# Attention and two MLPs on one core: keys and queries turned by VectorE, softmax sums spread through DRAM

## The chip, the cores and the metric

The kernel runs on one core of a Trainium2 chip. The metric is the device time of one execution in microseconds (us). A core has five engines that run side by side, each with its own instruction list in order: PE (TensorE, matmuls; PEld is its weight load), DVE (VectorE), ACT (ScalarE), POOL (GpSimd) and SP (SyncE, which here issues nearly all DMAs). They wait for each other by semaphores.

## The reference

Inputs are q, k, v (4 batches, 8 heads, 576 tokens, 64 wide), tau, and two pairs of MLP weights of 512x2048 and 2048x512.

```python
scores = scale * np.matmul(q, k.transpose(0, 1, 3, 2))
thresh = np.max(scores, axis=-1, keepdims=True) - tau
scores = np.where(scores >= thresh, scores, -1000000000.0)
attn = np.exp(scores - np.max(scores, axis=-1, keepdims=True))
attn = attn / (np.sum(attn, axis=-1, keepdims=True) + 1e-09)
x = np.matmul(attn, v)          # then (batch, token, head * width): 2304 x 512
h = x @ w_in                    # MLP 1: g = h >= 1: h; h <= -1: 0; else (h + 1)**2 / 4
x = g @ w_out
h = x @ moe2_w_in               # MLP 2: g = h * clip(h + 3, 0, 6) / 6
out = g @ moe2_w_out
```

## The kernel before

**Attention.** The 16 jobs are pairs of heads of one batch (job = 4 x batch + pair). A job's 576 queries go in five blocks, four of 128 and one of 64 (step t is one block, five steps a job). For each job `load_q` and `load_k` bring the two heads' rows to `qn`, `kn` with tokens on the partitions; `unit_q` and `unit_k` turn them on PE (five and six transpositions with `ident` into a pair of PSUM banks P0/P1, line 254) and ACT copies them to `qt`, `kt` (L266, L277; the copy of q also scales by `taus[:, 1:2]`, 0.125 where tau is not negative). A block is: `em_scores`, PE multiplies `qt` by `kt` into a P bank (L296), and DVE negates the scores to SBUF and keeps the row's smallest (L309); `em_exp`, ACT's exponential (L320), and DVE's threshold `th`, one instruction for each head (L322); `em_mask`, DVE zeroes what is beyond the threshold and sums the row into a column of `zt` (L328); `em_pt` and `em_tail`, PE turns the block's probabilities, nine transpositions into banks Q0/Q2 and Q3, from the moment MLP work is let in all into Q0, and ACT copies them out (L352, L355, L366, L370); `pv_chunk`, ten pairs of matmuls with `vn` into Q1 (L388), copied to `xu` by ACT (L394).

**The norm.** When a job's five blocks are summed, `pre_norm` takes the reciprocals `rz` (L408) and POOL spreads them 64 wide to `rb` (L412). Four steps later `em_norm` turns `rb` and `rz` on PE (five transpositions, L426 and L429) and DVE multiplies `xu` by the result (L431, L437). `xu` goes to DRAM (`xd`) and to the MLP.

**MLP 1 beside the attention.** Each f32 matrix is held as two f32r halves, so each product is three matmuls. `em_h` (L633) and `em_part` (L695) work on 256 tokens. The weights come as 64-bit numbers and are split by ACT, POOL and DVE (L116 to L139). The attention is a generator; from the step in which job 3's norm is done (`ready(0)`), each of its `yield` points adds 0.57 to a credit, and MLP 1 pieces are emitted while the credit is positive (L892 to L909). Behind the attention the rest of MLP 1 and MLP 2 run alone (L633 and L675).

**Order.** The program emits in this order, and a scheduler then places each engine's instructions by priority; some edges are set by hand (`after`). DMAs of SP run in SP's order: an issue that waits holds those behind it. `qn` and `kn` are single buffers, so the next job's load is issued when the turn of the present one has read them.

Of the kernel before, what the change touches and what calls it, by code (L numbers as in the profile page):

```python
# [18 lines left out]
def kernel(  # L19
# [12 lines left out]
    nc = tc.nc  # L32
# [15 lines left out]
    NF1 = 10  # L48
    MLAG = 2
# [161 lines left out]
    def rows(src):  # L211
        return src[0:MAIN, :].rearrange("(p c) d -> p c d", c=4)

    def load_q(j):
# [4 lines left out]
        for h in HEADS:  # L219
            src = q[b, 2 * hp + h]  # L220
            E.dma_start(out=qn[:, 0:4, h * D:(h + 1) * D], in_=rows(src))
            E.dma_start(out=qn[0:TAIL, 4, h * D:(h + 1) * D], in_=src[MAIN:SEQ, :])

    def load_k(j):
# [3 lines left out]
        for h in HEADS:  # L228
            src = k[b, 2 * hp + h]
            nc.sync.dma_start(out=kn[:, 0:4, h * D:(h + 1) * D], in_=rows(src))  # L230
# [3 lines left out]
    def load_v(j):  # L234
# [4 lines left out]
        for h in HEADS:  # L239
            src = v[b, 2 * hp + h]  # L240
            nc.sync.dma_start(out=t[:, 0:4, h, :], in_=rows(src))
# [16 lines left out]
    def unit_q(j):  # L258
        if j >= NJ or j in qt:
            return  # L260
        tm = unit_bank().rearrange("p e n -> p (e n)")
# [3 lines left out]
        qt[j] = ap.tile([128, SEQ], F32, tag="qt", name="qt", bufs=2)  # L265
        reads(S.activation(out=qt[j], in_=tm[:, 0:SEQ], func=ACTF.Copy, scale=taus[:, 1:2]))  # L266

    def unit_k(j):

        if j >= NJ or j in kt:  # L270
            return
        tm = unit_bank().rearrange("p e n -> p (e n)")
# [3 lines left out]
        kt[j] = ap.tile([128, SEQ + TAIL], F32, tag="kt", name="kt", bufs=2)  # L276
# [5 lines left out]
    def em_scores(j, i):  # L282
# [25 lines left out]
        for x, s in enumerate(ss):  # L308
            reads(V.tensor_scalar(out=p[:, x], in0=s[:, :, 0:HS], scalar1=-1.0, scalar2=3e38,  # L309
# [5 lines left out]
    def em_exp(j, i, x):  # L315
        p, nm, th, es = blk[j, i]
        if x >= (1 if i == NBLK - 1 else 2):
# [4 lines left out]
        V.tensor_scalar(out=th[:, x:x + 1], in0=nm[:, x:x + 1], scalar1=taus[:, 0:1], scalar2=None, op0=ALU.add)  # L322
# [17 lines left out]

    def em_pt(j, i, h):
# [5 lines left out]
        tm = bank("Q0" if mode["mlp"] or mode["n"] % 2 else "Q2")  # L347
# [10 lines left out]
    def em_tail(j, i):  # L358
# [4 lines left out]
        tl = bank("Q0" if mode["mlp"] else "Q3")  # L363
# [11 lines left out]
    def pv_chunk():  # L375
# [4 lines left out]
        if c == 0:  # L380
# [3 lines left out]
            o_t[j, g] = bank("Q1")  # L384
# [17 lines left out]
    def pre_norm(j):  # L402
# [14 lines left out]
    def em_norm(j):  # L417
# [5 lines left out]
        rz, rb = rbs.pop(j)  # L423
        bm = unit_bank().rearrange("p e n -> p (e n)")
# [580 lines left out]
```

## Time and profile before

| | |
|---|---|
| median of 3 runs | 1137.3 us (1137.07 to 1139.17) |
| span of the profiled execution | 1136.9 us |
| PE busy | 1108.0 us (97%) |
| PE weight load busy | 901.2 us (79%) |
| DVE busy | 575.6 us (51%) |
| ACT busy | 632.6 us (56%) |
| POOL busy | 404.3 us (36%) |
| DMA | 80.09 MB, mean 70 GB/s |

Busy times are shares of the whole span, but the program has stages with different loads, so they are read again for each stage below. An engine that is busy less than the bound can still hold it up, if a wait for it ends last. Matmuls overlap in PE, so the time that a group costs is read from the starts of its neighbours. The profiled execution's span and the runs' median differ by 0.4 us.

### The profile page before, as it was taken

To read this page: it belongs to the slowest core of one execution; us is meant where nothing else is said; L and a number is where in the kernel's file an instruction comes from. 1 tells how busy PE (TensorE), PEld (TensorE's weight loads), DVE (VectorE), ACT (ScalarE), POOL (GpSimd) and SP (SyncE) were. 2 spreads that over 40 slices of the span, in tenths; PEclk is the share of its full clock that TensorE was granted. 3 is DMA by queue.
4 is the path that set the end of the run, shared out by engine and by line. 5 is a ranking of instruction groups with operands and counts; after the bars stand their busy time and mean duration, and the time that the engine had idled before them with its cause. 6 is when DMAs were issued, how large, how long until landed. Compare 5 with 4: busy or idle time off the path is not lost.

```text
span 1136.9 us, 18024 instructions
## 1 busy us (share of the span) xinstructions
PE 1108.0 (97%) x6680; PEld 901.2 (79%) x6680; DVE 575.6 (51%) x1272; ACT 632.6 (56%) x1239; POOL 404.3 (36%) x383
## 2 busy tenths in 40 slices
PE   7998899999999999999999999999999999999998
PEld 5665567778777788788889988888888888898886
DVE  5888887766565565445545756557511111121111
ACT  5787987866666666556566766645432222333222
POOL 0222676411111111136645765557622222222221
PEclk8999999999999999999999999999999999999999
DMA  6434335222111210015322344533110110010001
GB/s 161 106 77 102 109 108 151 63 81 71 47 49 32 53 43 13 11 34 167 98 75 93 117 143 150 184 111 111 38 42 1 32 38 1 10 38 1 19 1 38
DMA packets 105368, 80.09 MB, mean 70 GB/s; under 512 B 66368, under 2 KB 90176, under 8 KB 105280
## 3 DMA queue, kind: packets, MB, share of 16 engines
q1 hardware_dynamic: 103920, 78.64, 23.9%
q8 instruction: 53, 0.87, 0.3%
q10 hardware_dynamic: 1360, 0.30, 0.1%
q14 instruction: 35, 0.29, 0.1%
HBM read 61.60 MB, written 17.30 MB: 69 GB/s over the span
## 4 chain that ended last, share of the span: by engine, by line
PE 88%; ACT 4%; DVE 4%; issue 1%; DMA 1%; POOL 1%; ACTq 0%; SPq 0%; DVEq 0%
PE Q L633 34%; PE P L675 27%; PE Q L695 7%; PE P L296 7%; PE Q L388 6%; PE Q L254 5%; DVE p L309 2%; ACT e L320 1%; PE P L254 1%; DVE p L328 1%; ACT Gf L352 1%; PE P L426 0%; POOL w_c L135 0%; DMA w_raw<-in_moe_w_in_dram 0%; DVE xl L617 0%
## 5 line engine op out<-in xcount | busy, mean ns | idle before, releaser
L651 POOL TENSOR_TENSOR gl<-r,gh 128x512 fp32r<-128x512 f32 (+1 forms) x190 | 203.3, 1071 | 548.4 <-ACT gh L650 547.9
L633 PE MATMUL Q<-xh,wih 128*128 128x512 f32 (+1 forms) x760 | 263.2, 346 | 2.5 <-DVE r L644 2.5
L633 PE MATMUL Q<-xh,wil 128*128 128x512 f32 (+1 forms) x760 | 257.0, 338 | 0.0
L633 PE MATMUL Q<-xl,wih 128*128 128x512 f32 (+1 forms) x760 | 256.8, 338 | 0.0
L647 DVE SCALAR_TENSOR_TENSOR r<-r,Q 128x512 f32<-128x512 f32 (+1 forms) x80 | 50.7, 634 | 249.0 <-ACT r L646 248.9
L650 ACT ACTIVATE gh<-r 128x512 fp32r<-128x512 f32 (+1 forms) x190 | 99.8, 526 | 126.2 <-PE P L675 53.3
L633 PEld LDWEIGHTS Q<-xh,wih 128*128 128x128 f32 x760 | 143.9, 189 | 25.0 <-issue 4.8
L633 PEld LDWEIGHTS Q<-xl,wih 128*128 128x128 f32 x760 | 143.9, 189 | 15.7
L633 PEld LDWEIGHTS Q<-xh,wil 128*128 128x128 f32 x760 | 143.8, 189 | 15.2
L646 ACT ACTIVATE r<-Q,three 128x512 f32<-128x512 f32 (+1 forms) x80 | 51.4, 643 | 143.7 <-PE Q L633 140.6
L309 DVE TENSOR_SCALAR_CACHE_REDUCE p<-P 128x576 f32<-128x576 f32 x144 | 104.3, 754 | 50.2 <-PE Q L254 32.0
L328 DVE SCALAR_TENSOR_TENSOR p<-p,th,e 128x576 f32<-128x576 f32 x144 | 121.3, 860 | 15.7 <-ACT e L320 14.9
L644 DVE SCALAR_TENSOR_TENSOR r<-r,Q 128x256 f32<-128x256 f32 (+1 forms) x110 | 55.0, 500 | 135.1 <-ACT r L643 127.7
L320 ACT ACTIVATE e<-p,nm 128x576 f32<-128x576 f32 x144 | 109.1, 774 | 25.4 <-DVE p L309 24.3
L254 PE MATMUL Q<-ident,p 128*128 128x128 f32 x656 | 109.8, 283 | 11.3 <-ACT Gf L352 4.9
L675 PE MATMUL P<-woh,gh 128*128 128x512 f32 x288 | 112.0, 390 | 0.6 <-DVE ob L733 0.6
L675 PE MATMUL P<-wol,gh 128*128 128x512 f32 x288 | 112.3, 390 | 0.0
L254 PEld LDWEIGHTS Q<-ident,p 128*128 128x128 f32 x656 | 74.5, 141 | 46.3 <-ACT Gf L352 12.7
L675 PE MATMUL P<-woh,gl 128*128 128x512 f32 x288 | 111.0, 390 | 0.0
L296 PE MATMUL P<-kt,qt 64*128 64x288 f32 (+1 forms) x640 | 100.5, 433 | 6.0 <-DVE p L309 4.9
L135 POOL TENSOR_TENSOR w_c<-w_c,w_raw 128x512 int32<-128x512 int32 x64 | 88.6, 1384 | 39.1 <-DVE w_c L133 22.7
L352 ACT ACTIVATE Gf<-Q 128x512 f32<-128x512 f32 x128 | 74.9, 594 | 40.0 <-PE Q L254 39.2
(84 smaller groups left out, 1865.1 us busy)
## 6 DMA issues: line engine op xcount, KB each, us to landing
w_raw<-in_moe_w_in_dram SPq DMA_DIRECT2D x32, 512.0 KB, 4.1
w_raw<-in_moe_w_out_dram SPq DMA_DIRECT2D x32, 512.0 KB, 3.7
kn<-in_k_dram SPq DMA_DIRECT2D x32, 128.0 KB, 2.6
vn<-in_v_dram SPq DMA_DIRECT2D x32, 128.0 KB, 2.9
x2p<-ob SPq DMA_DIRECT2D x16, 256.0 KB, 2.2
x2d<-ob SPq DMA_DIRECT2D x16, 256.0 KB, 4.1
xst<-x2d SPq DMA_DIRECT2D x16, 256.0 KB, 3.3
out_dram<-ob SPq DMA_DIRECT2D x16, 256.0 KB, 2.2
```

Source lines behind the costliest of these rows:

```text
L135: x = G.tensor_tensor(out=c.bitcast(I32), in0=c.bitcast(I32), in1=r, op=ALU.add)
L254: x = T.transpose(out, in_, ident)
L296: mm = T.matmul(o, qt[j][r, c], kt[j][r, k0:k0 + HS], start=True, stop=True, skip_group_check=True)
L309: reads(V.tensor_scalar(out=p[:, x], in0=s[:, :, 0:HS], scalar1=-1.0, scalar2=3e38, op0=ALU.mult, op1=ALU.min, accum_out=nm[:, x:x + 1]), ...
L320: pins["S"] = S.activation(out=e, in_=p[:, x], func=ACTF.Exp, bias=nm[:, x:x + 1], scale=-1.0)
L328: V.scalar_tensor_tensor(out=p[:, x], in0=p[:, x], scalar=th[:, x:x + 1], in1=e, op0=ALU.is_le, op1=ALU.mult, accum_out=zt[j][:, z:z + 1])
L352: S.activation(out=f[:, h, :, d0:d0 + 128], in_=tm.rearrange("p (c n) -> p c n", c=4), func=ACTF.Copy)
L633: mm = T.matmul(h, l[:, kk * 128:(kk + 1) * 128], r, start=(x == 0), stop=(x == 3 * KD - 1))
L650: x = S.activation(out=gh, in_=r, func=ACTF.Copy)
L651: y = G.tensor_tensor(out=gl, in0=r, in1=f32(gh), op=ALU.subtract)
L675: T.matmul(a, l, r, start=(first and x == 0), stop=(last and x == 2))
L695: mm = T.matmul(o, l, r, start=(f == fs[0] and x == 0 and i == 0), stop=(f == fs[-1] and x == 2 and i == 1), skip_group_check=True)
```

## The change

For batches two to four (`NAT = 1`: jobs 4 to 15) q and k are loaded as strips: each DMA fills 32 partitions with 32 of a head's 64 columns, in pieces of 128 bytes, and one DVE instruction turns all 32x32 blocks of q (576 wide), another of k (640 wide), straight into `qt` and `kt`. PE's transpositions and ACT's copies of these jobs go, and with them their use of the P banks. The scale moves to DVE's pass over the scores (a pointer to -0.125 in place of the number -1). The rows of these batches' v and of the output follow in the new token order.

For jobs 4 to 14 (`OVER`) the norm leaves PE: the 128x9 reciprocals are stored to DRAM turned, in pieces of 4 bytes, read back broadcast to 64 partitions each, and POOL multiplies `xu` by them in one instruction.

The two thresholds of a block become one DVE instruction. While MLP work is let in, `em_pt`, `em_tail` and `pv_chunk` all rotate through Q0 and Q1. Two branches of the attention's step for that time become one, with four `yield` points a step where a job had 22 in its five steps.

```diff
+    NAT = 1
     def zcol(x, c):
-        return 8 if c == NBLK - 1 else c // 2 * 4 + x * 2 + c % 2
+        return 8 if c == NBLK - 1 else x * 4 + c
+    OVER = range(HP, NJ - 1)
...
+    def strips(t, s0, src, h):
+        n = src.shape[0] // 32
+        flat = t.rearrange("p c n -> p (c n)")
+        for x in range(2):
+            p0 = 64 * h + 32 * x
+            nc.sync.dma_start(out=flat[p0:p0 + 32, 32 * s0:32 * (s0 + n)].rearrange("p (s d) -> p s d", d=32),
+                              in_=src[:, 32 * x:32 * x + 32].rearrange("(s p) d -> p s d", p=32))
...
     def unit_q(j):
+        qt[j] = ap.tile([128, SEQ], F32, tag="qt", name="qt", bufs=2)
+        if jobs[j][0] >= NAT:
+            V.transpose(out=qt[j], in_=qn.rearrange("p c n -> p (c n)")[:, 0:SEQ])
+            load_q(j + 1)
+            return
...
-        reads(S.activation(out=qt[j], in_=tm[:, 0:SEQ], func=ACTF.Copy, scale=taus[:, 1:2]))
+        reads(S.activation(out=qt[j], in_=tm[:, 0:SEQ], func=ACTF.Copy))
...
     def unit_k(j):
+        if jobs[j][0] >= NAT:
+            V.transpose(out=kt[j], in_=kn.rearrange("p c n -> p (c n)"))
+            load_k(j + 1)
+            return
...
-            reads(V.tensor_scalar(out=p[:, x], in0=s[:, :, 0:HS], scalar1=-1.0, scalar2=3e38,
+            reads(V.tensor_scalar(out=p[:, x], in0=s[:, :, 0:HS], scalar1=taus[:, 1:2], scalar2=3e38,
...
-        V.tensor_scalar(out=th[:, x:x + 1], in0=nm[:, x:x + 1], scalar1=taus[:, 0:1], scalar2=None, op0=ALU.add)
+        if x == n - 1:
+            V.tensor_scalar(out=th[:, 0:n], in0=nm[:, 0:n], scalar1=taus[:, 0:1], scalar2=None, op0=ALU.add)
...
+    def rotate():
+        mode["r"] = 1 - mode.get("r", 0)
+        return bank(f"Q{mode['r']}")
...
-        tm = bank("Q0" if mode["mlp"] or mode["n"] % 2 else "Q2")
+        tm = rotate() if mode["mlp"] else bank("Q0" if mode["n"] % 2 else "Q2")
...
-        tl = bank("Q0" if mode["mlp"] else "Q3")
+        tl = rotate() if mode["mlp"] else bank("Q3")
...
-            o_t[j, g] = bank("Q1")
+            o_t[j, g] = rotate() if mode["mlp"] else bank("Q1")
...
+        if j in OVER:
+            rd = dram.tile([9, 128], F32, name=f"rd{j}")
+            nc.sync.dma_start(out=rd.rearrange("c p -> p c"), in_=rz[:, :, 0])
+            for h in HEADS:
+                r = slice(64 * h, 64 * h + 64)
+                nc.sync.dma_start(out=rb[r, 0:MAIN].rearrange("p (c n) -> p c n", c=4),
+                                  in_=rd[4 * h:4 * h + 4, :].unsqueeze(0).to_broadcast([64, 4, 128]))
+                nc.sync.dma_start(out=rb[r, MAIN:SEQ], in_=rd[8:9, r].to_broadcast([64, 64]))
...
+        if j in OVER:
+            load_v(j + 2)
+            x = xu.pop(j)
+            G.tensor_tensor(out=x, in0=x, in1=rb, op=ALU.mult)
...
-            elif t < 35:
...
                 if t < n:
                     em_scores(*order[t])
                     maskq.append(order[t])
                     em_exp(*order[t], 0)
                     em_exp(*order[t], 1)
+                masked()
                 for x in now_at("z"):
                     pre_norm(*x)
-                masked()
                 yield
+                now = due(1)
+                for b in now:
+                    em_pt(*b, 0)
                 for x in now_at("n"):
                     em_norm(*x)
-                    yield
+                yield
+                pv_run(5)
                 tails(1)
-                pv_run(5)
                 yield
...
```

PE, last block of a job in the third quarter of the attention, before (`qn` are the next job's queries, `rb` and `rz` the former job's reciprocals, `p` the probabilities, the rest MLP 1):

```order
L254 MATMUL P_3574<-ident,qn 128x128 x5
L296 MATMUL P_3622<-kt,qt 64x288 x4
L254 MATMUL Q_3495<-ident,p 128x128 x4
...
L426 MATMUL P_3644<-ident,rb 128x128 x4
L429 MATMUL P_3644<-ident,rz 128x128
L254 MATMUL Q_3505<-ident,p 128x128 x4
L633 MATMUL Q_3501<-xh,wih_1344 128x256
```

The same place now (lines are those of the changed kernel, 323 the scores, 273 a turn, 645 and 707 MLP 1):

```order
L323 MATMUL P_3440<-kt,qt 64x288 x4
L273 MATMUL Q_3338<-ident,p 128x128 x4
L707 MATMUL Q_3198<-gh,woh_2773 128x256
L707 MATMUL Q_3198<-gl,woh_2773 128x256
L707 MATMUL Q_3198<-gh,wol_2774 128x256
L273 MATMUL Q_3380<-ident,p 128x128 x4
L645 MATMUL Q_3374<-xh,wih_1073 128x256
```

The turns of q and of the sums are gone, and those of k a little further on; the turns of `p` and the scores keep their places.

DVE at the same block, before (L431 and L437 are the norm's products, L407 and L408 the sums' reciprocals):

```order
L328 SCALAR_TENSOR_TENSOR p,z<-p,th,e 128x576 x2
L431 TENSOR_TENSOR xu<-xu,P_3644 128x512
L437 TENSOR_TENSOR xu<-xu,P_3644 64x64 x2
L309 TENSOR_SCALAR p,nm<-P_3622 128x576
L322 TENSOR_SCALAR th<-nm,taus 128x1
L644 SCALAR_TENSOR_TENSOR r<-r,Q_3501 128x256
L328 SCALAR_TENSOR_TENSOR p,z<-p,th,e 128x576
```

And now, in such a block (357 the mask, 336 the pass over the scores, 656 MLP 1):

```order
L357 SCALAR_TENSOR_TENSOR p,z<-p,th,e 128x576 x2
L282 STREAM_TRANSPOSE qt<-qn 128x576
L297 STREAM_TRANSPOSE kt<-kn 128x640
L656 SCALAR_TENSOR_TENSOR r<-r,Q_2854 128x256
L336 TENSOR_SCALAR p,nm<-P_3044,taus 128x576
L351 TENSOR_SCALAR th<-nm,taus 128x1
L357 SCALAR_TENSOR_TENSOR p,z<-p,th,e 128x576
```

Where the norm's products stood, the two block turns stand, one block ahead of the next job's first scores.

SP over one job late in the attention, before:

```order
L241 DMA vn_97<-in_v_dram 128x4x64 x2
L242 DMA vn_97<-in_v_dram 64x64 x2
L221 DMA qn<-in_q_dram 128x4x64
L222 DMA qn<-in_q_dram 64x64
...
L434 DMA xd_78<-xu 128x512
L438 DMA xd_80<-xu 128x64
L230 DMA kn<-in_k_dram 128x4x64
L232 DMA kn<-in_k_dram 64x64 x2
```

And now, from a job's loads of q to its last strip of k (`rd` is the sums' place in DRAM, 445 the store, 448 and 450 the broadcasts):

```order
L223 DMA qn<-in_q_dram 32x18x32 x4
L223 DMA kn<-in_k_dram 32x18x32 x2
L223 DMA kn<-in_k_dram 32x2x32 x2
L223 DMA kn<-in_k_dram 32x18x32
L445 DMA rd_2763<-rz 128x9x1
...
L448 DMA rb<-rd_2763 64x512
L450 DMA rb<-rd_2763 64x64
...
L223 DMA kn<-in_k_dram 32x2x32
```

The store and the broadcasts stand between the strips of k, so the last strip is issued behind a wait for the store's landing.

## Rows read from the trace of the kernel before

**Rows 1.** The page, part 1: busy us, share of the span, instructions.
```profile
PE 1108.0 (97%) x6680; PEld 901.2 (79%) x6680; DVE 575.6 (51%) x1272; ACT 632.6 (56%) x1239; POOL 404.3 (36%) x383
```

**Rows 2.** Busy time by stage: start:end, length, each engine's busy us.
```profile
core 0: us, PE busy (x) PEld busy (x) DVE busy (x) ACT busy (x) POOL busy (x), PEclk, DMA share, GB/s
0.00:109.00 109.00, 97.57 (x696) 65.45 (x697) 87.30 (x260) 81.15 (x163) 20.10 (x35) 0.97 0.42 108
109.00:212.00 103.00, 93.56 (x693) 69.61 (x692) 85.87 (x211) 85.23 (x183) 65.69 (x63) 1.00 0.43 122
212.00:472.00 260.00, 256.87 (x1998) 206.23 (x1996) 157.99 (x465) 171.68 (x369) 39.62 (x59) 1.00 0.18 46
472.00:1137.00 665.00, 659.96 (x3303) 559.90 (x3299) 244.40 (x339) 294.55 (x525) 278.93 (x227) 1.00 0.21 66
```

**Rows 3.** PE's waits, 109 to 472 us: us in total, times, longest.
```profile
PE Q L254 <- ACT Gf L352: 4.6, 6, 1.5
...
PE Q L254 <- ACT Gt L366: 1.4, 3, 0.6
...
PE Q L254 <- ACT Gf L355: 0.8, 1, 0.8
```

**Rows 4.** PE in order of time, 300 to 312 us: start, us, instructions.
```profile
300.93 0.71 PE L254 MATMUL P<-ident,qn 128*128 128x128 f32 x5
301.57 1.19 PE L296 MATMUL P<-kt,qt 64*64 64x288 f32 x8
...
304.26 0.60 PE L426 MATMUL P<-ident,rb 128*128 128x128 f32 x4
...
304.81 0.60 PE L254 MATMUL Q<-ident,p 128*128 128x128 f32 x4
...
309.30 0.82 PE L254 MATMUL P<-ident,kn 128*128 128x128 f32 x6
309.96 0.60 PE L254 MATMUL Q<-ident,p 128*128 128x128 f32 x4
```

**Rows 5.** Groups by shape, 109 to 472 us: count, busy us, mean ns, idle before.
```profile
L254 PE MATMUL P<-ident,kn 128*128 128x128 f32 x60 | 8.7, 272 | 0.0
```

**Rows 6.** Groups by shape over the whole span, same columns.
```profile
L651 POOL TENSOR_TENSOR gl<-r,gh 128x512 fp32r<-128x512 f32 x98 | 130.6, 1333 | 270.4 <-ACT gh L650 270.1
...
L328 DVE SCALAR_TENSOR_TENSOR p<-p,th,e 128x576 f32<-128x576 f32 x144 | 121.3, 860 | 15.7 <-ACT e L320 14.9 <-ACT Gt L366 0.3
...
L322 DVE TENSOR_SCALAR th<-nm,taus 128x1 f32<-128x1 f32 x144 | 25.3, 207 | 0.4
...
L266 ACT ACTIVATE qt<-P,taus 128x576 f32<-128x576 f32 x16 | 11.8, 739 | 1.4 <-PE P L254 1.4
...
L277 ACT ACTIVATE kt<-P 128x640 f32<-128x640 f32 x16 | 11.2, 703 | 1.1 <-PE P L254 1.0
...
L431 DVE TENSOR_TENSOR xu<-xu,P 128x512 f32<-128x512 f32 x16 | 11.0, 685 | 16.7 <-PE P L429 10.8 <-ACT xu L394 5.8
```

**Rows 7.** Single lines: ns min/median/max, first and last start in us.
```profile
L408 DVE RECIPROCAL rz<-z x9: 210/216/216, 212.1 to 472.1; 128x9 f32<-128x9 f32 x9
...
L230 SPq DMA_DIRECT2D kn<-in_k_dram x32: 572/588/703, 0.7 to 409.8; - x32
```

**Rows 8.** POOL and DVE in order of time, 126.5 to 130 us.
```profile
127.21 1.78 POOL L139 TENSOR_TENSOR wol<-w_c,woh 128x512 fp32r<-128x512 f32 x1
...
127.80 1.82 DVE L328 SCALAR_TENSOR_TENSOR p<-p,th,e 128x576 f32<-128x576 f32 x1
```

**Rows 9.** DMA issues: count, KB each, median us from issue to landing.
```profile
kn<-in_k_dram SPq DMA_DIRECT2D x32, 128.0 KB, 2.6
...
kn<-in_k_dram SPq DMA_DIRECT2D x64, 16.0 KB, 2.3
...
taus<-in_tau_dram ACTq DMA_DIRECT2D x1, 0.5 KB, 2.9
```

More of the change, by code (lines that the diff above doesn't have):

```diff
@@ L209, with rows @@
     qt, kt = {}, {}
-    def rows(src):
+    def rows(src, b):
+        if b >= NAT:
+            return src[0:MAIN, :].rearrange("(c p) d -> p c d", c=4)
         return src[0:MAIN, :].rearrange("(p c) d -> p c d", c=4)
+    def strips(t, s0, src, h):
[5 more added lines that the diff above has]
+                              in_=src[:, 32 * x:32 * x + 32].rearrange("(s p) d -> p s d", p=32))
     def load_q(j):
@@ L220, in load_q @@
             src = q[b, 2 * hp + h]
-            E.dma_start(out=qn[:, 0:4, h * D:(h + 1) * D], in_=rows(src))
+            if b >= NAT:
+                strips(qn, 0, src, h)
+                continue
+            E.dma_start(out=qn[:, 0:4, h * D:(h + 1) * D], in_=rows(src, b))
             E.dma_start(out=qn[0:TAIL, 4, h * D:(h + 1) * D], in_=src[MAIN:SEQ, :])
@@ L229, in load_k @@
             src = k[b, 2 * hp + h]
-            nc.sync.dma_start(out=kn[:, 0:4, h * D:(h + 1) * D], in_=rows(src))
+            if b >= NAT:
+                strips(kn, 2, src, h)
+                strips(kn, 0, src[MAIN:SEQ, :], h)
+                continue
+            nc.sync.dma_start(out=kn[:, 0:4, h * D:(h + 1) * D], in_=rows(src, b))
             for r in range(2):
@@ L240, in load_v @@
             src = v[b, 2 * hp + h]
-            nc.sync.dma_start(out=t[:, 0:4, h, :], in_=rows(src))
+            nc.sync.dma_start(out=t[:, 0:4, h, :], in_=rows(src, b))
             nc.sync.dma_start(out=t[h * TAIL:(h + 1) * TAIL, 4, h, :], in_=src[MAIN:SEQ, :])
@@ L316, in em_exp @@
         p, nm, th, es = blk[j, i]
-        if x >= (1 if i == NBLK - 1 else 2):
+        n = 1 if i == NBLK - 1 else 2
+        if x >= n:
             return
@@ L423, in em_norm @@
         rz, rb = rbs.pop(j)
+        if j in OVER:
+            load_v(j + 2)
+            x = xu.pop(j)
+            G.tensor_tensor(out=x, in0=x, in1=rb, op=ALU.mult)
+            done_jobs.add(j)
+            if b < NB - 1:
+                nc.sync.dma_start(out=xd[b][:, hp, :], in_=x[:, 0:MAIN])
+            nc.sync.dma_start(out=xd[NB][:, hp, b * TAIL:(b + 1) * TAIL], in_=x[:, MAIN:SEQ])
+            return
         bm = unit_bank().rearrange("p e n -> p (e n)")
@@ L569, in attention @@
                     unit_q(*x)
-                    yield
-                for b in now:
-                    em_pt(*b, 0)
-                    yield
-                pv_run(5)
                 for b in now:
@@ L737, in fin_out @@
             b, r = divmod(c, MAIN // 128)
-            nc.sync.dma_start(out=out[b * SEQ:b * SEQ + MAIN, :].rearrange("(p c) d -> c p d", c=4)[r], in_=ob)
+            if b >= NAT:
+                dst = out[b * SEQ + r * 128:b * SEQ + r * 128 + 128, :]
+            else:
+                dst = out[b * SEQ:b * SEQ + MAIN, :].rearrange("(p c) d -> c p d", c=4)[r]
+            nc.sync.dma_start(out=dst, in_=ob)
         else:
```

52 lines of the change are left out of this document (8 added, 44 removed).

## The prediction, made before the changed kernel was run

> **What bounds the kernel now.** First the page's busy times: PE works 1108.0 us of the 1136.9 us span, the other engines 36 to 56% [rows 1]. The reader is to see that only PE can be the bound as an average. Second, the same by stage, since the change touches one stage alone [rows 2]: to 109 us jobs 0 to 4 of the attention run alone; from 109 to 212 us jobs 5 to 7 run beside the first MLP pieces, and the weights are split there; from 212 to 472 us jobs 8 to 15 run beside MLP pieces with the weights ready; then MLP alone. PE idles 11.4, 9.4, 3.1 and 5.0 us in them. In the third stage PE is busy 99% while DVE and ACT are at 61 and 66%: a PE microsecond removed there is a microsecond of the kernel. In the second DVE and ACT are both busy 83%, in the first 80 and 74% with little else for PE to do: there a shorter PE list can turn into PE waiting. In the last stage PE has nothing to gain or lose but its work. The granted clock is 1.00 from 109 us on. Third, the waits: of PE's idle time from 109 to 472 us, 4.6 + 1.4 + 0.8 = 6.8 us were ended by ACT copying a turned block out of its bank [rows 3].
>
> **Time on the span.** The rows are of an execution with a span of 1136.9 us; the median of the runs is 1137.3, so 0.4 us lies around it. The sum below is a difference and is taken from 1137.3.
>
> **PE work that goes.** 12 jobs (4 to 15) lose 5 turns of q and 6 of k, 11 jobs (4 to 14) lose the 5 turns of the norm: 187 turns. What a turn costs is read from starts, not from durations: from the start of a group to the start of what follows it are 301.57 - 300.93 = 0.64 us for q, 309.96 - 309.30 = 0.66 for k and 304.81 - 304.26 = 0.55 for the norm [rows 4]. So 12 x 1.30 + 11 x 0.55 = 21.7 us. The durations of single turns mislead: 60 turns of k have a mean of 272 ns but keep PE busy 8.7 us together, 145 ns each, because they overlap [rows 5]. The Trainium skill (TensorE: Matmul & The Clock Gate, Part 4: PE-mode transpose) gives about 275 ns for a transposition inside a kernel; the trace agrees with that as a duration, 272 ns, and by it the sum would be 187 x 0.275 = 51 us and the time 1086, an estimate that the starts speak against.
>
> By stage: q and k of jobs 4 and 5 fall before 109 us (2.6 us); q and k of jobs 6 to 8 and the norms of 4 to 6 in the second stage (3 x 1.30 + 3 x 0.55 = 5.6 us); q and k of 9 to 15 and the norms of 7 to 14 in the third (7 x 1.30 + 8 x 0.55 = 13.5 us). I take the third whole. Of the second I take half, 2.8 us, between none (DVE and ACT set the pace) and all. Of the first I take nothing, between 0 and 2.6: there PE waits for DVE, and DVE gets longer. Sum 16.3 us: **1121.0 us**.
>
> **What must hide for that.** *DVE* gets two turns of 32x32 blocks a job, 576 and 640 wide. No row shows one. The nearest is the two-input pass of 512 at 685 ns [rows 6], which scales to 0.77 + 0.86 = 1.6 us; with twice the rate of the mask (860 ns for 576) it is 1.7 + 1.9 = 3.6. I take 1.6, since a plain pass from SBUF to SBUF is nearest to the first row. It loses four threshold instructions of 207 ns and the norm's product, 0.69, so 1.5 a job. Scaling the scores by a pointer in place of -1 may cost something: ACT's copy with a pointer takes 739 ns for 576, without one 703 for 640, which bounds it at 0.11 x 9 = 1.0 us a job. DVE's load in the third stage is 158.0/8 = 19.8 us a job of 32.5 (8 jobs from 212.1 to 472.1 [rows 7]); after it is 19.9 to 22.9 of 30.8. It is hidden there. *ACT* loses two copies, 0.74 + 0.70 = 1.4 us a job: 20 of 30.8. *POOL* trades two small broadcasts for one product of 576, 1.5 us by its row for 512 (1333 ns). It is idle 85% of the third stage, but it shares something with DVE: beside a POOL pass of 1.78 us one DVE mask took 1.82 us where 860 ns is the mean [rows 8]. So each product may cost DVE up to 1.0 us, 11 us in all, and nothing of it on PE's path while DVE has 8 us a job to spare. *SP*: a job issues 4 q, 8 k, 5 for the sums, 4 v and 2 stores, 23 where 16 were; at 588 ns [rows 7] that is 4.1 us more, 13.5 of 30.8.
>
> **The two banks.** Turns now alternate between Q0 and Q1. A turn no longer waits for the copy of the one just before it, so up to 6.8 us can go [rows 3]; but the PV group now takes one of the two banks for its whole length and its copy (685 ns at most, by the DVE row of the same size) stands before the second turn after it: 23 groups stand there in the order, x 0.69 = up to 16 us. PE has MLP matmuls to put between. I take 0, ends of a gain of 7 and a loss of 16, and expect nearer the first.
>
> **Fewer stops for the MLP.** A job now has 20 points at which MLP work is let in, not 22, with 0.57 a point. The orders show it: of the MLP's matmuls 1320 stood among the attention's, now 1179. The 141 others run behind the attention, where PE idles 0.8%. So this is worth nothing by itself; what it costs is cover: a shorter attention with less MLP in it has fewer PE instructions to fill a wait with. In the second stage this is what could eat the other half.
>
> **Rivals.** *All of it and the waits too.* If the free banks take the 6.8 us of copy waits away and stages one and two give their whole share, 21.7 + 6.8: 1108.8. For it: ACT, which ends those waits, loses 1.4 us a job. Against: DVE and ACT at 83% in the second stage.
>
> *DVE and ACT become the bound.* With the block turn at 3.6, the pointer at 1.0 and the POOL product at 1.0, DVE in the second stage goes from 85.9/3 = 28.6 to 32.7 us a job of 34.3, so PE cannot get through faster there, and in the third to 23.9 of 30.8, where each late mask now meets less MLP cover. Then stage two gives nothing and stage three half: -6.8, 1130.5.
>
> *SP holds the keys back (slower).* One mechanism: the sums of a job are stored to DRAM in 1152 pieces of 4 bytes, and SP waits for their landing, L, before it issues their broadcast; the last k strips stand behind that on SP, and DVE turns k in order, so a late strip stops DVE, the scores and PE. From one turn of k to the next are 30.8 us. SP reaches the store after about a block, 6.1 us, issues it (0.6), waits L, issues 4 broadcasts and the last strip (3.0), which lands in 2.6: 12.3 + L. It decides from L = 18.5 us. Rows: 64 pieces (16 KB) land in 2.3 us, 512 pieces (128 KB) in 2.6, and 128 pieces of 4 bytes in 2.9 [rows 9]. By the first pair 1152 pieces cost 0.8 more, L = 3.1; by the last, 0.6/128 each, L = 7.7. Both are far from 18.5. Beyond it each us costs 11: L = 21 gives 27.5 back and 1148.5. The Trainium skill (VectorE: DVE Perf Modes, The three transpose paths) warns that a plain DMA that transposes by strides is 19 times slower than the DMA's own transposition. That speaks against exactly this store; the rows' 2.9 us for pieces of 4 bytes do not, and no run here shows the other path. By 19 times the 2.3 us row L would be 44 us, 25.5 beyond the point, and the time about 1400; of the 0.08 below I give that 0.02.
>
> *It does nothing.* The 16.3 us come back as PE waits of the same length in stages two and three, 1137. It needs about 1 us a job that nothing above names.
>
> **How the numbers follow.** Forecast as worked (1114 to 1127, by the half of stage two, the first stage and a few us for the banks): 0.57. All and the waits (1107 to 1113): 0.15. DVE and ACT the bound (1128 to 1134): 0.16. Nothing: 0.04. SP slower: 0.08. A measurement tells 0.2%, 2.3 us, from no change. So faster 0.88, same 0.04, slower 0.08. The range goes from 1109 to 1131, the ends of the second and third case; it leaves out the slower case, nothing, and parts of two.
>
> **What would show it.** Right: 187 fewer turns; the job in the third stage near 30.8 us by the reciprocals; PE at 98% or more there; the block turns under 1 us each; the sums' store landing under 8 us; q and k landed long before DVE turns them. Wrong: PE waits on the block turns' DMA; block turns of 1.7 us; PE idle from 109 to 212 us well over 9.4 us (the half I gave stage two is gone) or copy waits of PV's bank of more than some us.

## The result, and the profile after

The changed kernel takes 1144.2 us (median of 4 runs, 1142.6 to 1146.6), the kernel before 1137.6 (4 runs): ratio 1.006, interval 1.0048 to 1.0073. It is slower by 7 us, where the forecast was 16 us faster; the time lies above the range. The profiled execution has a span of 1144.8 us, 7.9 more than the 1136.9 of before.

PE did lose work. The page's busy times, beside [rows 1]: 1091.8 us in place of 1108.0, 16.2 less. So its idle time grew by 24.1.

```profile
PE 1091.8 (95%) x6493; PEld 884.3 (77%) x6493; DVE 589.5 (51%) x1199; ACT 614.4 (54%) x1215; POOL 411.9 (36%) x372
```

The busy times by stage answer [rows 2]. The borders are the reciprocals of jobs 4, 7 and 15, as there (109.5, 212.1 and 472.1 us before).

```profile
core 0: us, PE busy (x) PEld busy (x) DVE busy (x) ACT busy (x) POOL busy (x), PEclk, DMA share, GB/s
0.00:111.90 111.90, 97.21 (x685) 62.93 (x685) 91.93 (x249) 78.04 (x158) 19.09 (x34) 1.00 0.47 111
111.90:229.10 117.20, 89.80 (x626) 66.94 (x625) 86.12 (x187) 78.18 (x169) 64.25 (x58) 0.90 0.50 111
229.10:465.70 236.60, 232.37 (x1785) 183.11 (x1785) 163.52 (x421) 156.93 (x348) 47.09 (x50) 0.99 0.27 58
465.70:1144.80 679.10, 672.42 (x3406) 571.34 (x3402) 247.98 (x345) 301.30 (x542) 281.49 (x231) 1.00 0.21 65
```

Stage one is 2.4 us longer than before, stage two 14.6, stage three 23.4 shorter, the MLP alone 14.3 longer (the deferred matmuls). Stage three with what follows gains 9.1 us. The loss is in stage two: PE idles 27.4 us of 117.2, where it idled 9.4 of 102.6, and its granted clock is 0.90 where it was 1.00. PE's waits there, beside [rows 3], as total, times, longest; below them ACT's two longest:

```profile
PE Q L273 <- ACT Gf L385: 14.9, 3, 9.2
PE P L323 <- DVE p L336: 3.9, 5, 1.4
PE Q L421 <- ACT Gf L385: 3.9, 1, 3.9
```

```profile
ACT w_raw L117 <- DMA w_raw<-in_moe_w_in_dram: 10.7, 2, 9.7
ACT w_c L120 <- POOL wil L140: 5.9, 1, 5.9
```

PE waits for ACT's copy of a turned block. In the longest of these waits ACT, which works in order, stands before it at a weight that has not landed. The chain of waits there, in order of time (start, us):

```profile
147.21 10.30 DMA rd<-rz
157.52 0.46 SPq L448
158.03 0.59 SPq L450
158.67 0.59 SPq L448
...
159.37 4.93 DMA w_raw<-in_moe_w_in_dram
164.32 0.05 ACT w_raw L117
...
165.51 0.49 ACT Gf L385
```

PE's row behind it, with the 9.2 us it had waited:

```profile
166.06 0.47 PE L273 MATMUL Q<-ident,p 128*128 128x128 f32 x1 [9.23 <-ACT Gf L385]
```

The store of the sums is issued at 147.21, and its first broadcast only 10.3 us later. The weight load stands behind on SP, lands at 164.3, and PE starts again at 166.1. The second longest wait, 5.4 us up to 135.6, comes by another way: POOL, in order too, stands at job 4's product until the late broadcast lands, the split of a weight (`wil`, L140) stands behind the product, and ACT waits for this split:

```profile
131.04 1.40 POOL L469 TENSOR_TENSOR xu<-xu,rb 128x576 f32<-128x576 f32 x1 [6.96 <-DMA rb<-rd]
133.69 0.67 ACT L120 ACTIVATE w_c<-w_raw 128x512 f32<-128x512 f32 x1 [5.87 <-POOL wil L140]
135.57 1.97 PE L273 MATMUL Q<-ident,p 128*128 128x128 f32 x8 [5.37 <-ACT Gf L385]
```

SP's wait over the whole span:

```profile
SPq L448 <- DMA rd<-rz: 109.2, 11, 11.7
```

### The profile page after: what moved, and what is told of

It reads as the page before. It is cut to its first block, busy times and chain, and to the rows that moved or that the text cites. A ratio compares the mean times of both kernels' runs of the same rounds, so it can differ in the third digit from the quotient of the medians.

```text
span 1144.8 us, 17591 instructions
## 1 busy us (share of the span) xinstructions
PE 1091.8 (95%) x6493; PEld 884.3 (77%) x6493; DVE 589.5 (51%) x1199; ACT 614.4 (54%) x1215; POOL 411.9 (36%) x372
## 4 chain that ended last, share of the span: by engine, by line
PE 77%; DVE 9%; ACT 4%; issue 3%; DMA 3%; POOL 2%; SPq 1%; ACTq 0%; DVEq 0%; POOLq 0%
PE Q L645 31%; PE P L687 27%; PE P L323 5%; PE Q L707 5%; PE Q L421 4%; PE Q L273 4%; DVE p L357 3%; DVE p L336 3%; DMA rd<-rz 1%; DVE w_c L134 1%; POOL w_c L136 1%; ACT e L348 1%; DMA kn<-in_k_dram 1%; DVE w_c L128 1%; DMA w_raw<-in_moe_w_out_dram 1%
## 5 line engine op out<-in xcount | busy, mean ns | idle before, releaser
L336 DVE TENSOR_SCALAR_CACHE_REDUCE p<-P,taus 128x576 f32<-128x576 f32 x144 | 113.1, 813 | 49.0 <-PE Q L273 38.5
```

## The experiments

Spans and medians are in us. Each kernel ran beside the kernel before, whose medians were 1136.0 to 1137.6. The last column is the ratio to it, with its interval.

| run | median | ratio |
|---|---|---|
| changed kernel | 1144.2 | 1.0060 (1.0048-1.0073) |
| e1 norm on PE | 1133.0 | 0.9961 (0.9946-0.9976) |
| e2 sums over DRAM from job 8 | 1128.6 | 0.9925 (0.9911-0.9940) |
| e3 store in rows | 1130.0 | 0.9936 (0.9919-0.9952) |
| e4 broadcasts two steps later | 1137.3 | 0.9999 (0.9989-1.0009) |
| e5 both movements from job 8 | 1127.3 | 0.9913 (0.9899-0.9928) |
| e6 hold without small pieces | 1131.7 | 0.9949 (0.9932-0.9966) |
| e7 small pieces without hold | 1143.1 | 1.0052 (1.0037-1.0067) |
| e8 old order and banks | 1142.4 | 1.0047 (1.0030-1.0064) |
| e9 old banks | 1147.9 | 1.0088 (1.0073-1.0103) |
| e10 small pieces from ACT's queue | 1144.7 | 1.0065 (1.0050-1.0080) |
| e11 order and banks alone | 1138.4 | 1.0006 (0.9997-1.0016) |
| e12 sums turned, store in rows | 1129.5 | 0.9935 (0.9919-0.9952) |
| e13 e5 with the literal | 1132.4 | 0.9969 (0.9955-0.9984) |
| e14 e12 with the literal | 1129.5 | 0.9944 (0.9929-0.9958) |
| e15 512 small pieces | 1142.2 | 1.0057 (1.0041-1.0073) |
| e16 small pieces spread | 1129.4 | 0.9931 (0.9914-0.9948) |
| e17 128 small pieces | 1138.3 | 1.0012 (1.0001-1.0024) |
| e18 e12 with block turns from job 8 | 1132.5 | 0.9957 (0.9942-0.9971) |

In e3, e6, e7, e10, e15, e16 and e17 the sums come back from DRAM in another order, so the product takes other rows' sums: these kernels answer a question and could not replace the kernel.

### First question: is it the store of the sums?

Theory A: SP's wait for the store holds up the weights. Theory B: the new order, the two banks or the block turns on DVE make the waits.

```diff
e1
-    OVER = range(HP, NJ - 1)
+    OVER = range(0)
e2
+    OVER = range(2 * HP, NJ - 1)
e3
-            nc.sync.dma_start(out=rd.rearrange("c p -> p c"), in_=rz[:, :, 0])
+            nc.sync.dma_start(out=rd.rearrange("c p -> (c p)").rearrange("(p c) -> p c", c=9), in_=rz[:, :, 0])
```

> The changed kernel with the norm back on TensorE for all jobs: no store of the sums, no broadcasts, no product on POOL; the turns of q and k stay on VectorE, and the new order of a step and the two banks stay. Theory A (SP waits about 10 us for each store of the sums, the weight loads stand behind it, ACT waits in order for the weights and PE for ACT): the wait is gone, so PE's idle time from 111.9 to 229.1 us, 27.4 us in the changed kernel, falls back to about 10; the time is the changed kernel's 1144.2 less these 18 us and some of the lower clock there, plus 11 norms of 0.55 us on PE: about 1127 us. Theory B (the shorter attention, its new order of a step or the shared two banks make PE wait in this stretch, whatever SP does): the idle time stays above 20 us and the time between 1140 and 1150 us.

> The changed kernel with the sums sent over DRAM only from job 8 on, when the attention's weights are loaded and split; jobs 4 to 7 norm on TensorE as before. Theory A (the store's landing harms only where weight loads stand behind it on SP): all 8 stores that remain are hidden in the third stage, which stays at about 29.6 us a job; the second stage's PE idle time falls from 27.4 to about 10 us; 4 norms of 0.55 us come back on PE: about 1123 us, below both kernels. Theory B (order of a step, banks, or block turns on VectorE): about as slow as the changed kernel, 1140 to 1147 us.

> The changed kernel with one access pattern of the store changed: the sums are written as 128 pieces of 36 bytes in place of 1152 pieces of 4 bytes, so the sums come back from DRAM in another order (the product takes another row's sum); every instruction, its place and its size stay. Theory A (the price is the landing of 1152 small pieces): SP's wait per store falls from about 10 us to 2 to 4 us, the weights land in time, PE's idle time from 111.9 to 229.1 us falls from 27.4 to 10 to 14 us, the granted clock there goes back to 1.00, and the time is about 1121 us, between 1118 and 1128. Theory B (order, banks, block turns): the wait on SP falls as well, but PE's idle time and the time stay, 1140 to 1147 us. If the landing is slow for any store to DRAM that is read at once, and not for its pieces, SP's wait stays near 10 us and so does the time.

Measured: 1133.0, 1128.6 and 1130.0. All three fall by 11 to 16 us, so theory B is out as the cause of the slowdown. e3 is the cleanest: every engine's instructions stand in the same order as in the changed kernel, and nothing but the pieces of the store differs. Its stage two:

```profile
111.50:213.80 102.30, 86.07 (x624) 64.72 (x624) 88.78 (x186) 78.46 (x169) 64.85 (x58) 0.97 0.48 127
```

It is 14.9 us shorter than in the changed kernel. 11.2 of these are PE's idle time (16.2 for 27.4); 3.7 are PE's busy time for nearly the same matmuls (86.1 us for 624, where 626 took 89.8), at a granted clock of 0.97 for 0.90. In the changed kernel the clock shows the lower level, 0.50 (1.2 of 2.4 GHz), from 135 to 147 us and from 161 to 171 us; both times it fell while PE stood in one of the two waits above (5.4 and 9.2 us). e1, e2 and e3 came out 6, 6 and 9 us above the times expected of theory A (1127, 1123 and 1121); that remainder is the fourth question.

### Second question: SP standing still, or the pieces?

e4 emits the broadcasts two steps later. e6 keeps SP's hold with no small pieces, e7 has the pieces and no hold.

```diff
e4
+                for x in now_at("m"):
+                    bcast(*x)
e6 (on e3)
+            for n in range(3):
+                rn = dram.tile([9, 128], F32, name=f"rd{j}_{n}")
+                nc.sync.dma_start(out=rn.rearrange("c p -> (c p)").rearrange("(p c) -> p c", c=9),
+                                  in_=rd.rearrange("c p -> (c p)").rearrange("(p c) -> p c", c=9))
+                rd = rn
e7 (on e3, behind the broadcasts)
+            spare = dram.tile([9, 128], F32, name=f"sp{j}")
+            nc.sync.dma_start(out=spare.rearrange("c p -> p c"), in_=rz[:, :, 0])
```

> The changed kernel with the broadcasts of a job's sums issued two steps after the store in place of right behind it; the store keeps its 1152 pieces of 4 bytes. In job 5 the two weight loads of w_in then stand ahead of SP's wait, in job 6 two loads of w_out do; everything else is like the changed kernel. Theory A (the harm is SP standing before the weight loads, not the landing itself): the 4.9 to 10.7 us for which ACT waits for the weights go, PE's idle time from 111.9 to 229.1 us falls from 27.4 to 10 to 16 us: 1121 to 1130 us. Theory B (the landing itself loads the DMA engines, or order, banks, block turns): 1140 to 1147 us.

> SP held back, the DMA engines not: the kernel with the store in 128 pieces of 36 bytes (1130.0 us; SP waits about 2 us for it), and behind it three copies of these 4.5 KB from DRAM to DRAM, each reading what the one before wrote, so that the broadcasts start some 8 to 10 us later, as in the changed kernel, while the DMA engines have almost nothing to do for it (sums in another order, as there). If SP standing still is the harm: weights late, about 1140 to 1145 us. If it is the 1152 pieces on the DMA engines: about 1131 to 1133 us.

> The DMA engines loaded, SP not held: the kernel with the store in 128 pieces of 36 bytes (1130.0 us), and behind the broadcasts a second store of the sums in 1152 pieces of 4 bytes to a place that nobody reads, so that SP goes on at once (sums in another order, as there). If SP standing still is the harm: 1130 to 1132 us. If the pieces occupy the DMA engines so that what is issued behind them lands late, as the two weight loads did that were issued 2.8 us behind the store and landed 10.9 us later where 3.9 is usual: about 1136 to 1145 us, with SP's wait near 2 us.

Measured: 1137.3, 1131.7 and 1143.1. As the whole cause theory A falls. In e4 the weight loads of job 5 stand ahead of SP's wait, and half of the loss remains; in e7 SP waits 8.1 us in all for the stores that it needs (109.2 in the changed kernel), and nearly all of the loss remains. The loads themselves are late. The same load of w_in in the chain of waits, as start and us to landing, in e3, e4 and e7:

```profile
144.12 3.99 DMA w_raw<-in_moe_w_in_dram
```

```profile
146.54 10.88 DMA w_raw<-in_moe_w_in_dram
```

```profile
150.85 11.99 DMA w_raw<-in_moe_w_in_dram
```

In e4 it follows the small pieces by 2.8 us, in e7 by 4.3. In the changed kernel SP issues it only after the pieces have landed, and it takes 4.9 us; from the store of job 5's pieces to the landing of this load it is 17.1 us there, 16.3 in e7 and 13.7 in e4, where from e3's store in rows it is 8.1. So with these pieces in the way the load gains only 0.8 to 3.4 us from being issued early. POOL's product of job 4 waits the same 7.0 us for its broadcasts in e7, though SP issues them 1.7 to 3.5 us behind the pieces. The last two columns of e7's busy times in slices of 2 us, the DMA share and GB/s, show the stop (its second store is issued at 146.58, the broadcasts from 149.01):

```profile
149.00:151.00 2.00, 1.79 (x16) 1.55 (x15) 0.83 (x3) 1.27 (x3) 0.73 (x2) 1.00 0.06 0
151.00:153.00 2.00, 1.80 (x12) 0.94 (x11) 1.97 (x6) 2.00 (x6) 1.08 (x1) 1.00 0.00 0
153.00:155.00 2.00, 2.00 (x19) 2.00 (x18) 2.00 (x4) 0.80 (x2) 1.66 (x1) 1.00 0.10 13
155.00:157.00 2.00, 0.97 (x9) 0.73 (x7) 2.00 (x5) 0.00 (x0) 1.36 (x2) 1.00 0.05 6
157.00:159.00 2.00, 0.00 (x0) 0.00 (x0) 0.26 (x2) 0.00 (x0) 0.00 (x0) 1.00 0.42 49
159.00:161.00 2.00, 0.00 (x0) 0.00 (x0) 0.00 (x0) 0.00 (x0) 0.00 (x0) 0.87 0.86 222
```

Broadcasts and a weight load of 512 KB are issued, and until 157 us next to nothing moves, some 10 us from the store. e6 is weaker evidence than planned: in stage two its broadcasts start 9.1 to 10.5 us behind the store (9.2 to 12.9 in the changed kernel), but a weight load stands between the copies. So a hold of about this length that lets loads through cost 1.7 us (1131.7 for e3's 1130.0), and the two intervals overlap; what a hold over all loads would cost was not tried.

### Third question: what in the pieces stops the DMAs?

e10 is e7 with the second store issued from ACT. e15 stores 512 small pieces in place of 1152 in the changed kernel (SP waits for both parts), e17 is e7 with 128. e16 is e7 with the pieces 64 bytes apart in DRAM in place of 4; the instructions of e7, e16 and e17 stand in the same order on every engine.

```diff
e10 (on e7)
-            nc.sync.dma_start(out=spare.rearrange("c p -> p c"), in_=rz[:, :, 0])
+            nc.scalar.dma_start(out=spare.rearrange("c p -> p c"), in_=rz[:, :, 0])
e15
+            nc.sync.dma_start(out=rd[0:4, :].rearrange("c p -> p c"), in_=rz[:, 0:4, 0])
+            nc.sync.dma_start(out=rd[4:9, :].rearrange("c p -> (c p)").rearrange("(p c) -> p c", c=5), in_=rz[:, 4:9, 0])
e16 (on e7)
+            spare = dram.tile([9, 128, 16], F32, name=f"sp{j}")
+            nc.sync.dma_start(out=spare[:, :, 0].rearrange("c p -> p c"), in_=rz[:, :, 0])
e17 (on e7)
+            nc.sync.dma_start(out=spare[0:1, :].rearrange("c p -> p c"), in_=rz[:, 0:1, 0])
```

> Like the run in which a second store of 1152 pieces of 4 bytes, read by nobody, followed each job's broadcasts on SP's queue (1143.1 us; the DMA engines then show 0.00 to 0.10 of busy share for some 6 us, while a weight load issued behind it waits); here that second store goes out from ScalarE's queue (sums in another order, as there). If a store of small pieces stops only what stands behind it in its own queue: 1130 to 1133 us, with an issue of 0.4 to 1.3 us a job on ScalarE. If it stops the DMA engines whichever queue it came from: 1140 to 1145 us.

> The changed kernel with 4 of the 9 columns of sums stored in 512 pieces of 4 bytes, the other five in 128 pieces of 20 bytes (sums in another order); SP waits for both. With 1152 pieces SP waited 10 to 11 us for the landing, with 128 pieces of 36 bytes about 2. If the stop goes with the number of pieces: 2 + 8.5 x (512 - 128)/(1152 - 128) = 5 to 6 us a store and 1131 to 1137 us. If any store of 4-byte pieces takes its 10 us whatever their number: 1143 to 1146 us.

> The kernel with a second store of the sums in 1152 pieces of 4 bytes that nobody reads (1143.1 us), with the pieces 64 bytes apart in DRAM in place of 4; every instruction and its place are the same. If pieces that lie side by side in the same stretch of DRAM hinder each other: the stop shrinks and the time comes near the 1130.0 us without the second store, 1130 to 1135. If writing 4 bytes is what is slow, wherever they go: 1141 to 1146 us.

> The same kernel with one of the nine columns in the second store: 128 pieces of 4 bytes side by side, in place of 1152. By the forecast's pricing (0.6 us for 128 pieces) the store lands in about 3 us and the time is 1130 to 1133 us. If the stop is set by pieces that share a stretch of 512 bytes (128 of them in each column) and columns go side by side, not one after the other: 8 us of stop also here, 1141 to 1145 us.

Measured: 1144.7, 1142.2, 1129.4 and 1138.3. The same load of w_in in e10, e17 and e16:

```profile
152.17 9.37 DMA w_raw<-in_moe_w_in_dram
```

```profile
148.48 10.07 DMA w_raw<-in_moe_w_in_dram
```

```profile
144.87 4.11 DMA w_raw<-in_moe_w_in_dram
```

From ACT's queue the pieces stop SP's loads as well: SP's own store in rows, issued 0.4 us ahead of them, takes 4.9 us there. Fewer pieces help little: with 512 SP's broadcasts in stage two come 8.2 to 11.0 us behind the store, and with 128 some 8 of e7's 13 us of loss are still there. e17's slices (its second store is issued at 144.54) show the same stop, the DMA share next to last:

```profile
146.50:148.50 2.00, 2.00 (x18) 1.80 (x17) 0.36 (x1) 0.80 (x2) 1.01 (x2) 1.00 0.00 0
150.50:152.50 2.00, 2.00 (x19) 1.61 (x16) 1.97 (x5) 1.27 (x4) 1.19 (x1) 1.00 0.02 9
```

The distance decides: in e16 the same 1152 pieces of 4 bytes, 64 bytes apart, cost nothing (1129.4 against e3's 1130.0). Its two stores (count, KB, median us to landing), and its DMAs behind a pair issued at 139.81 and 140.20:

```profile
rd<-rz SPq DMA_DIRECT2D x11, 4.5 KB, 2.0
sp<-rz SPq DMA_DIRECT2D x11, 4.5 KB, 3.3
```

```profile
143.00:145.00 2.00, 0.61 (x3) 0.42 (x3) 0.00 (x0) 2.00 (x5) 1.19 (x2) 1.00 0.17 60
145.00:147.00 2.00, 2.00 (x15) 1.40 (x16) 1.80 (x5) 2.00 (x6) 0.84 (x2) 1.00 0.51 155
```

So 128 or more 4-byte pieces written side by side into DRAM stop the core's DMAs for some 8 to 10 us; neither their count nor their size alone does it. (The nine columns are farther apart in e16 too; e17, which has one column, stops as well, so it is the pieces within a column.) How near is too near was not tried, nor whether the distance itself counts or how many pieces fall into one stretch of DRAM, and what stands still inside no row shows. e3's pieces of 36 bytes lie side by side too and land in about 2 us. The Trainium skill (DMA: Bandwidth & Descriptors, Specifications) says that transfers under 512 bytes make the DMA read, modify and write; if that alone made the stop, e16 and e3 would have stopped as well, so the measurement narrows it. The same page of the Trainium skill (Back-pressure in remote DMA) says, of copies between cores, that stalled writes stall the other queues of the DMA engine that they come from; e10 fits that, with writes to DRAM (9.37 us for SP's load), but no row shows which writes stall.

### Fourth question: where is the rest of the forecast?

e12 mends the change with its sums in the right order, e11 has all that is not the two data movements, e8 the movements (sums from job 8) without the order and the banks, e9 has the new order and old banks; in e8 a step's two branches stand as in the kernel before.

```diff
e12
+            V.transpose(out=t32, in_=rz32)
+            nc.sync.dma_start(out=rd.rearrange("c (b i) -> b c i", b=4), in_=t32)
e11
-    NAT = 1
+    NAT = NB
-    OVER = range(HP, NJ - 1)
+    OVER = range(0)
e9 (on e2)
-        tm = rotate() if mode["mlp"] else bank("Q0" if mode["n"] % 2 else "Q2")
+        tm = bank("Q0" if mode["mlp"] or mode["n"] % 2 else "Q2")
...
-            o_t[j, g] = rotate() if mode["mlp"] else bank("Q1")
+            o_t[j, g] = bank("Q1")
e8 (on e9)
+            elif t < 35:
...
```

> The kernel with the sums over DRAM from job 8 on (1128.6 us), but with the order of a step and the three banks of the kernel before in stages two and three; block turns on VectorE from job 4 as changed. If the new order and the two banks bring nothing by themselves (forecast: 0, +7/-16 us): 1126 to 1131 us, the 141 matmuls back in the attention. If they make the waits on the score pass in stage two (5.1 us, where the kernel before has 1.6): about 1124 us. If they are what lets TensorE run at 98.6% in stage three: 1133 to 1137 us, with waits on Gf copies of some us back.

> The kernel with the sums over DRAM from job 8 on (1128.6 us) with its new order of a step, but the three fixed banks of the kernel before (turned blocks in Q0, the PV group in Q1). The old order with the old banks took 1142.4. If the two shared banks carry that gain: 1138 to 1143 us, with waits for Gf copies back in stage three. If the order of a step carries it: 1127 to 1131 us. My forecast had 0 for the banks, between 7 gained and 16 lost.

> The new order of a step, the two banks, one threshold a block and the pointer alone: q, k and the norm on TensorE in all jobs, as in the kernel before (1137.4 us). Block turns and late sums with the old order took 1142.4, with the new one 1128.6. If the order and the banks bring their 13.8 us by themselves: about 1124 us, plus what the 187 turns cost there. If they bring it only because VectorE and SP do the turning (TensorE has no wait to fill otherwise): 1135 to 1140 us. Least likely, the turns of q and k in the shared order cost more than before: above 1141.

> The whole change with its sums in the right order and no small pieces: VectorE turns the sums in blocks of 32x32 (128x32, one instruction a job), and the store writes 128 pieces of 128 bytes. If the 4-byte pieces are all that is wrong with the change: as with the pieces of 36 bytes, 1128 to 1132 us, SP waiting about 2 us for each store, TensorE's idle time in stage two near 16 us. If any store that is read back at once harms: above 1138.

Measured: 1142.4, 1147.9, 1138.4, 1129.5. e12 is the cure: the small turn takes DVE 210 ns a job, and SP's waits for the 11 stores are 9.2 us in all. The others show a product, not a sum:

| | order and banks of before | new order and banks |
|---|---|---|
| turns and norm on PE | 1137.6 | 1138.4 (e11) |
| block turns, sums from job 8 | 1142.4 (e8) | 1128.6 (e2) |

The new order alone brings nothing, the movements alone cost 5 us, together they bring 9. And with the new order but one fixed bank for the turns (e9) it is 19 us worse than e2. PE's waits of e9 in stage two, and of e2 below:

```profile
PE Q L273 <- ACT Gt L399: 6.5, 5, 4.6
PE Q L273 <- ACT Gf L385: 4.3, 5, 2.2
```

```profile
PE Q L273 <- ACT Gf L385: 1.7, 2, 1.2
...
PE Q L273 <- ACT Gt L399: 0.4, 1, 0.4
```

A turn that must wait for ACT to empty the one bank finds less to do before it. That the removed turns of q, k and the norm used to stand in these gaps is argued from this, not shown by itself. It is also not the whole of it: of the 17.1 us between the spans of e9 and e2, 5.9 are PE's idle time and 11.2 its busy time, part of this at a lower clock (0.92 for 0.97 in stage two); where the rest of the busy time comes from stays open.

e5 starts both movements at job 8. e13 and e14 give the score pass of the jobs turned on PE its literal back and scale q in ACT's copy again. e18 is e12 with block turns from job 8.

```diff
e5, e13, e18
-    NAT = 1
+    NAT = 2
e13, e14
-            reads(V.tensor_scalar(out=p[:, x], in0=s[:, :, 0:HS], scalar1=taus[:, 1:2], scalar2=3e38,
+            reads(V.tensor_scalar(out=p[:, x], in0=s[:, :, 0:HS], scalar1=taus[:, 1:2] if jobs[j][0] >= NAT else 1.0, scalar2=3e38,
```

> Both data movements of the change from job 8 on alone: q and k of batches three and four by block turns on VectorE (batch two on TensorE as before), sums over DRAM from job 8; the new order of a step and the banks stay. Theory A1 (after the sums' store is out of the way, what is left missing of the forecast is VectorE in the first two stages: in job 3's 24 us, where the kernel before took 20.9, VectorE idles 1.4 us): stage one goes back from 111.9 to about 109.5 us; in stage two 6 us of turns come back on TensorE but its waits for VectorE's score pass, 5.1 us, go; about 1125 us. Theory B1 (the order of a step makes the waits): stage one stays near 112 and stage two grows by the turns put back: 1130 to 1133 us.

> The kernel with both data movements from job 8 on (1127.3 us), where the jobs turned on TensorE (0 to 7) scale q by the pointer in ScalarE's copy, as before, and their score passes take a literal, 1.0. A score pass with the pointer takes 813 ns, with a literal 754: 9 passes a job, 0.53 us. If stage one waits for VectorE's score passes: 4 jobs x 0.53 = 2.1 us, stage one back from 111.5 to 109.4 us, and up to as much in stage two: 1123 to 1126 us. If the pointer is hidden there and the block turns or the threshold cause the loss: 1127 us as before.

> The kernel with the sums turned by VectorE and stored in 128 pieces of 128 bytes (1129.5 us), with the literal in the score passes of jobs 0 to 3 and the scale in ScalarE's copy of q there. Stage one's first three jobs lose 0.53 us each, job 3 has two pairs of block turns besides (24.0 us where the kernel before took 20.9): stage one 109.6 to 110.2 us, 1127 to 1128.5 us in all. If the pointer is hidden: 1129.5.

> Block turns of q and k from job 8 on, sums turned by VectorE and stored in 128 pieces of 128 bytes from job 4 on. Against the kernel with both from job 8 on (1127.3 us) 4 norms of 0.55 us leave TensorE in stage two: 1125 to 1127 us if they count, 1127 to 1129 if TensorE waits for VectorE there as with the block turns in (1129.5).

Measured: 1127.3, 1132.4, 1129.5, 1132.5. In e5 stage one stays at 111.5 us, so taking the block turns out of it brings next to nothing by itself, against theory A1. Stage one in e12, e11 and e13:

```profile
0.00:111.70 111.70, 96.91 (x686) 62.65 (x686) 91.92 (x250) 77.93 (x158) 19.23 (x37) 1.00 0.47 111
```

```profile
0.00:111.30 111.30, 97.31 (x700) 64.04 (x701) 89.59 (x243) 81.19 (x164) 20.47 (x35) 1.00 0.41 106
```

```profile
0.00:109.70 109.70, 97.43 (x700) 64.03 (x701) 87.28 (x242) 81.37 (x164) 20.11 (x35) 1.00 0.41 107
```

It is 111.3 with all turns on PE, and 109.7 once the literal is back: where all turns of stage one are on PE, the pointer is its loss. e13's score passes show its price, 60 ns:

```profile
L336 DVE TENSOR_SCALAR_CACHE_REDUCE p<-P,taus 128x576 f32<-128x576 f32 x72 | 56.3, 813 | 39.8 <-PE Q L273 38.0 <-PE P L323 1.5
L336 DVE TENSOR_SCALAR_CACHE_REDUCE p<-P 128x576 f32<-128x576 f32 x72 | 52.2, 753 | 13.9 <-PE P L323 10.7 <-PE Q L273 2.5
```

As a whole e13 and e18 miss: 5 us above e5, mostly in stage two (105.6 and 102.2 us for 100.1) and in the MLP alone (681.8 and 681.6 for 679.2). The edits let the scheduler place PE's instructions of stage two otherwise; what in that costs the time stays open. e14's gain in jobs 0 to 3 (0.9 us by then) is given back in job 4, which DVE turns and whose passes keep the pointer: its stage one ends at 111.7 us, as e12's does. **e5 has the lowest median: 1127.3 us, 0.9913 (0.9899 to 0.9928) of the kernel before, and 17 us under the changed one.** The intervals of e2 and e12 overlap its own.

## Why the prediction was wrong, point by point

- **The store's landing, "Both are far from 18.5".** This step failed, twice. First the size: the bound of 3.1 to 7.7 us was priced by the piece from loads, one of them of 128 pieces of 4 bytes [rows 9]. SP waits 10 us for it, and in e17 already 128 pieces, written side by side, stop the DMAs about as long, where the row of the load has 2.9 us: the price of a load did not carry over to this store. Second the condition: 10 us is still far from 18.5, and the store cost 15 us all the same, because others than the keys waited.
- **Who stands behind it.** The rival named the mechanism's place, SP, and looked only at the k strips. The keys were nearly in time (DVE waited 4.7 us for them in the whole span, none of it in stage three). Those who came late were the weight loads, which no sentence of the prediction mentions, and POOL's product, for which it allowed time on DVE and none for waiting. In the changed kernel they stood behind SP's wait; e7, where SP goes on, shows that their data does not move in that time either. So the slower rival had the right store, a wrong victim, and a point of 18.5 us that did not matter. By the Trainium skill (VectorE: DVE Perf Modes, The three transpose paths), a store transposed by strides would be 19 times slower than the DMA's own path, and I made 44 us of that, an estimate from the time of a plain load; measured are 10 us, five times the 2.0 of the store in rows. Its warning pointed the right way, and 0.02 was too little for it.
- **Stage two, "I take half, 2.8 us".** It got 14.6 us longer. Without the stop (e12) it gets 0.9 shorter: 101.7 us, PE idle 16.9 us, of which 7.7 wait for DVE's score pass, where before it was 1.6. The prediction's worry about DVE at 83% was right and half was too much.
- **Stage one, "I take nothing".** 2.2 to 2.4 us longer. From e12's 111.7 us, taking out the block turns alone brought 0.2 (e5, 111.5), the pointer of jobs 0 to 3 alone nothing (e14, 111.7), both together 2.0 (e13, 109.7): not a sum either. The prediction had the pointer's price (at most 0.11 us a pass; 0.06 measured) and wrote that PE waits for DVE there and that DVE gets longer, and still bounded the stage between 0 and 2.6 us of gain: its own reason named a loss.
- **Stage three, 13.5 us whole.** Right in kind: the stops cost only about 2 us there and behind it, and only one weight load is issued in that stage. In e12 stage three and the tail gain 11.2 us, and PE's busy time falls by 11.9 in them. Over the whole span it falls by 21.5, where 21.7 were taken, and by 17.8 against e11, which has the new order with the turns on PE: the price of the turns was right to within a fifth.
- **Two banks, "I take 0".** With the removed turns gone they are worth 19 us (e9 against e2), where the bound allowed a gain of 7. The prediction treated order, banks and turns as terms of a sum.
- **The deferred MLP, "worth nothing by itself".** Right: in e11 stage three is 10.0 us shorter than before and the MLP alone 13.6 longer, with 4.0 us gained in the two stages ahead, and the span is the same within 0.4.
- **Right:** the two block turns, 0.77 and 0.81 us (1.6 taken), and POOL's product, 1.49 (1.5 taken), beside [rows 5, 6]:

```profile
L297 DVE STREAM_TRANSPOSE kt<-kn 128x640 f32<-128x640 f32 x12 | 9.7, 809 | 4.7 <-DMA kn<-in_k_dram 4.7
L282 DVE STREAM_TRANSPOSE qt<-qn 128x576 f32<-128x576 f32 x12 | 9.3, 774 | 1.1 <-PE P L323 0.5 <-DMA qn<-in_q_dram 0.5
...
L469 POOL TENSOR_TENSOR xu<-xu,rb 128x576 f32<-128x576 f32 x11 | 16.4, 1488 | 28.1 <-ACT xu L427 14.8 <-DMA rb<-rd 13.3
```

Summed by spans for e12: +2.2, -0.9 and -11.2 make -9.9 us, where 0, -2.8 and -13.5 made -16.3. The store makes the other 17.8 us to the profiled span of 1144.8; by the medians it is 14.7 (1144.2 for 1129.5).

## What to carry to other kernels

When a change adds a DMA that writes small pieces side by side, ask which other DMAs are under way in that stage and who needs them first, not only who waits for its result; turn the data on chip first, so that pieces are 128 bytes (e12, 210 ns), or keep it out of stages that load weights (e2). Price a store from a store, not from a load. And when work is taken out of an engine's list, try the order and the banks of the rest together with it: here each half alone brought nothing or cost time.

## What was new about the hardware

- 1152 writes of 4 bytes into DRAM, 4 bytes apart, hold their reader for some 10 us; 64 bytes apart they land after 3.3 (e16), and the same 4.5 KB in 128 pieces of 36 bytes lands after 2.0.
- Such writes stop DMAs from another queue too (e10: the load of w_in on SP takes 9.37 us behind a store issued by ACT).
- A pass from PSUM with a pointer for its factor takes 60 ns longer than with a literal (813 for 753 ns, 576 wide).
- DVE turns 128x640 f32 in 32x32 blocks in 0.81 us, and 128x32 in 0.21.
